# A long-convolution branch run between the matmuls of a gated MLP: its k·v transform shares a slot with an inverse transform, and its slots are dealt anew

## The chip, the core and the metric

The kernel runs on one core of a Trainium2 chip. The time is the device time of one execution in microseconds. Before the change it is 1860.31 us, the median of three runs (1859.35 to 1860.98).

## What is computed

Forward and backward pass of a layer with two branches over S = 2048 rows and D = 1024 channels, in bf16:

```python
xn = layernorm(x)
# A: a gated long convolution along the rows, one channel at a time
k_shift = sum(k_pad[:, t:t+S] * shift_k[:, 3-t] for t in range(4))      # four taps
kv = k_shift * v
y  = irfft(rfft(kv, 2S) * rfft(ssm_k, 2S))[:S] + kv * ssm_D
# B: a gated MLP, F = 3584
h  = relu(xn @ W_gate) * (xn @ W_up)
out = x + xn * y + h @ W_down
```

The outputs are `out` and its gradients for x, k, v, the four taps, ssm_k, ssm_D and the three weights.

## The kernel before

**Two branches on one TensorE.** Branch B (class `LnMlp`) is a sequence of matmuls of 128x128 weights by 512 columns, called large matmuls here: `hidden` (gate, up and the gradient of h: three GEMMs of 8 large matmuls for each tile of 128 rows, 14 blocks of eight row tiles), then `grad_down` and `grad_in` (weight gradients, GEMMs of 16), `out_phase` and `grad_x`. Twice, in the first block of `grad_down` and at the seam to `grad_in`, `four` runs four GEMMs of 16 interleaved, so four accumulators are open at once; PSUM has eight tiles in all (`ps_tile`, a pool of 8).

**Branch A as slots.** Branch A (class `ABranch`) does the convolution and its gradients for eight groups of 128 channels. `slots` is a generator, written out by hand, that yields pairs: a piece of matmul work (or None) and a piece of VectorE work (or None). The main loop hands out large matmuls, and when `SLOT` = 1900 ns of them have been handed out (`DENSE` = 1900 or 1250 ns in `grad_down` and `grad_in`, the shorter one after a slot without matmuls) it places the next slot. All of it is kept in program order on every engine, so what stands first in a queue runs first.

**What a group does.** Transforms are done as two matrix steps with a 32x32 block transpose on VectorE between them (`flip`, two instructions of 128x1024). First steps are `fwd1` and `fwd1_filter` (eight matmuls for half of the row tiles' columns, 512 columns each, on 32-row tiles of the array, written into PSUM tiles `ps_c`); second steps are `f2`, `f2_pair`; inverses are `inv_a`, `inv_a_pair` (four quarters for a pair of spectra) and then `inv_b`. Every PSUM tile is cast by ScalarE (`act`, L87) into the arena. `cmul` is a complex product of two spectra, ten VectorE instructions. `taps` computes the four taps in seven VectorE steps. `inv_b` needs the flip of what the inverse wrote; `f2_pair` of the next group needs the flips of both its inputs (`flip_B`).

**Crossed blocks.** `joint` issues jobs of different row tiles in turn, so that they run side by side in the array. `crossed` puts two row tiles of an inverse and the two others of a forward first step into one such block, and the reverse into a second one. Before the change it is used for the filter's first step (with `inv_a`) and for the gated gradient's, `Bg` (with quarters 0 and 1 of `inv_a_pair`). The k·v first step, `f1k`, stands alone as two blocks at the end of a group.

**Loads.** `fetch` queues a load, one queued load is issued on SP's queue after each slot (`steps`), none while `hold` is set in the last rows of a block, and `need` issues at once. The stores of B's results (`ru`, `ht`) are deferred by two GEMMs (`defer`, `tick`) and issued on the same queue. The pools `e2` (tiles `ru`) and `e1` (`ht`, `gh`) have six buffers each.

Of the kernel before, what the change touches and what calls it, by code (L numbers as in the profile page):

```python
# [48 lines left out]
class ABranch:  # L49
# [59 lines left out]
    def open(self):  # L109
        R = "right"  # L110
        self.con = self.pool("a_con", 1, side=R)
        self.lng = self.pool("a_lng", 1, side=R)
        self.ld = self.pool("a_ld", 1, side=R)
        self.ts = self.pool("a_ts", 3, side=R)
        self.tmp = self.pool("a_tmp", 2, side=R)
        self.xp = self.pool("a_xt", 1, side=R)
        self.sm = self.pool("a_sm", 2, side=R)
        self.big = self.pool("a_big", 3, side=R)
        self.lnx = self.pool("a_lnx", 5, side=R)

    def open_arena(self):
        for _ in range(2):
            self.pools.pop().release()
        arena = self.pool("a_are", 1, side="right").tile([P, 8, NB1 * P], BF16, name="arena")
        self.flp = arena[:, 0:2, :].rearrange("p e (k c) -> p e k c", c=P)
# [6 lines left out]
        self.Bh = arena[:, 6, :].rearrange("p (b x cp n i) -> p b x cp n i", x=2, cp=16, n=NB1, i=2)  # L132
        self.Bg, self.Bk, self.H, self.GKV = rows(7), rows(6), spectrum(4), spectrum(7)
        self.Cg, self.Ch, self.Cy = half(5), half(5), half(6)
# [6 lines left out]
    def tables(self):  # L141
# [28 lines left out]

        it = self.ts.tile([P, 2, NB1], I32, name="itR", tag="ts")
        tr = self.ts.tile([P, 2, NB1], F32, name="trR", tag="ts")
        hold(nc.gpsimd.iota(it[:], pattern=[[0, 2], [4, NB1]], base=1, channel_multiplier=0))
# [24 lines left out]
        V.tensor_scalar(out=wI[:], in0=itW[:], scalar1=q32[:], scalar2=None, op0=ALU.add)  # L198
        itN = self.ts.tile([P, 1, NB1], F32, name="itN", tag="ts")
        itNi = self.ts.tile([P, 1, NB1], I32, name="itNi", tag="ts")  # L200
        hold(nc.gpsimd.iota(itNi[:], pattern=[[0, 1], [1, NB1]], base=0, channel_multiplier=0))
# [49 lines left out]
    def store_time(self, ap2d, cg, t):  # L251
        for u in range(2):
            self.store(self.tview(ap2d, cg)[u], t[64 * u:64 * u + 64, 0:16, :])

    def ttile(self, name):
        return self.ts.tile([P, 19, P], BF16, name=name, tag="ts")

# [12 lines left out]
    def load_filter(self, st):  # L270
        st["hn"] = self.ld.tile([P, 2, 32, NB1], BF16, name="hn")
        self.load_rows(st, 0)
        self.later(self.load_rest, st)
# [15 lines left out]
    def load_xn(self, st):  # L289
        xt = st["xt"] = self.xp.tile([P, 16, P], BF16, name="xt")  # L290
        self.load_time(xt, self.xn_d, st["cg"])
# [4 lines left out]
    def load_k(self, st):  # L296
        nc = self.nc
        kp = st["kp"] = self.lng.tile([P, 19, P], BF16, name="kp")
        self.pri.now()
        self.tc.keep_in_program_order(nc.gpsimd.memset(kp[0:1, 0:3, :], 0.0))  # L300
        kv = self.tview(self.k, st["cg"])
        self.load_time(kp[:, 3:19, :], self.k, st["cg"])
        self.load(kp[64:P, 0:3, :], kv[0, :, 13:16, :])
        self.load(kp[1:64, 0:3, :], kv[1, 0:63, 13:16, :])
# [189 lines left out]

    def crossed(self, inv, fwd):

        I, F = inv[0], fwd[0]
        return [self.joint(I[0][0:1], I[1][0:1], F[2], F[3]), self.joint(F[0], F[1], I[2][0:1], I[3][0:1])] + inv[1][1:]

# [75 lines left out]
    def steps(self):  # L575
# [12 lines left out]
        yield 3400  # L588
        self.load_k(st)
        self.load_taps(st)  # L590
        yield 3400
        self.load_g(st)
        yield 3400
        self.load_v(st)
        yield 6800
        self.load_xn(st)
        self.pin = False
        self.pri.strict = True
        self.open_arena()
        self.begin(st)  # L600
        for st in self.sts:
# [15 lines left out]
    def start_kvt(self, st):  # L617
        kvt = st["kvt"] = self.ttile("kvt")
        self.tt(kvt[:, 0:16, :], st["ksh"][:], st["vt"][:], ALU.mult)

# [18 lines left out]
    def first(self, st):  # L639
        tk, f1h, nx = st["tk"], self.fwd1_filter(st)[1], self.ahead(st, 1)  # L640
        yield f1h[0], None
        yield None, tk
        yield f1h[1], tk
        self.fetch(nx, self.load_filter)
        yield None, self.both(lambda: self.add_D(st), tk)
        yield None, tk
        flH = self.flip_H()
        yield None, flH
        yield None, flH
        yield None, tk  # L650
        yield None, tk
        f2H = [(1, self.f2(self.H, 1, j)) for j in range(4)]
        yield f2H[0:2], lambda: self.gate_grad(st)
        self.fetch(nx, self.load_xn)
        yield None, tk
        yield f2H[2:4], lambda: self.start_kvt(st)
        yield None, None
        f1g, f1k = self.fwd1(self.Bg, st["gt"])[1], self.fwd1(self.Bk, st["kvt"])[1]
        yield f1g[0], None
        yield None, None  # L660
        yield f1g[1], None
        self.fetch(nx, self.load_g)
        yield None, None
        yield f1k[0], None
        flG = self.flip_B(self.Bg, 0)
        yield None, flG
        yield f1k[1], flG
        yield None, None
        flK = self.flip_B(self.Bk, 1)
        yield None, flK  # L670
        yield None, flK
        yield None, None

    def slots(self, st, gi):
# [28 lines left out]
        if last:  # L703
            iaG = [iaG[1][0], None, iaG[1][1]]
        else:
            self.need(self.load_filter, nx)
            self.need(self.load_rest, nx)
            iaG = self.crossed(iaG, self.fwd1_filter(nx))
        yield iaG[0], q
# [3 lines left out]
        yield None, lambda: self.turn(H, 1, 1)  # L713
        self.fetch(n2, self.load_filter)
        q = self.cmul(K, G, True, G, 0)
# [27 lines left out]
        yield [], lambda: self.halo(st)  # L743
        self.fetch(nx, self.load_k, self.load_taps)
        ia = self.inv_a_pair()
        if last:
            ia = [ia[1][0], None] + ia[1][1:]
        else:
            self.need(self.load_xn, nx)
            yield None, lambda: self.gate_grad(nx)  # L750
            self.fetch(n2, self.load_xn)
            ia = self.crossed(ia, self.fwd1(self.Bg, nx["gt"]))
        yield None, None
        q = self.cmul(K, G, True, G, 1)
        yield ia[0], q
        yield None, q
        yield None, q
        yield ia[1], q
        yield None, q
        q = self.cmul(H, K, False, K, 1)  # L760
        self.fetch(n2, self.load_g)
        yield None, q
        yield ia[2], q
        yield None, q
        yield None, q
        yield None, q
        gk = self.ttile("gk")
        tg = self.taps(st, gk, gks, [(0, 0), (1, 1), (2, 2), (3, 3)])
        yield None, tg
        yield None, tg  # L770
        yield ia[3], tg
        yield None, tg
        yield ia[4], tg
        yield None, tg
        f2H = [] if last else [(1, self.f2(H, 1, j)) for j in range(4)]
        yield f2H[0:2], tg
        self.store_time(self.out_gk, st["cg"], gk)
        fly = self.flip_C(self.Cy, 0)
        yield None, fly
        yield None, fly  # L780
        tk = None
        if not last:
            self.need(self.load_k, nx)
            self.need(self.load_taps, nx)
            self.begin(nx)
            tk = nx["tk"]
        yield None, tk
        yield None, tk
        yield f2H[2:3] + self.inv_b(st, "yt", 0), tk
        self.store_time(self.y_d, st["cg"], st["yt"])  # L790
        flh = self.flip_C(self.Ch, 0)
        yield None, flh
        yield None, flh
        yield None, tk
        yield None, tk
        yield f2H[3:4] + self.inv_b(st, "gh", 0), tk
        yield None, tk
        yield None, None
        if last:
            yield None, lambda: self.store_gh(st)  # L800
            return
        self.need(self.load_v, nx)
        yield None, lambda: self.start_kvt(nx)
        f1k = self.fwd1(self.Bk, nx["kvt"])[1]
        yield None, lambda: self.store_gh(st)
        flG = self.flip_B(self.Bg, 0)
        yield f1k[0], None
        yield None, flG
        yield f1k[1], flG
        yield None, None  # L810
        flK = self.flip_B(self.Bk, 1)
        yield None, flK
        yield None, flK
        yield None, None
        yield None, None
# [4 lines left out]
class LnMlp:  # L820
# [7 lines left out]
    def open_left(self):  # L828
# [3 lines left out]
        self.w2 = tc.alloc_tile_pool(name="b_w2", bufs=1, side="left")  # L832
        self.e2 = tc.alloc_tile_pool(name="b_e2", bufs=6, side="left")
        self.e1 = tc.alloc_tile_pool(name="b_e1", bufs=6, side="left")
        self.ps = tc.alloc_tile_pool(name="b_ps", bufs=8, space=bass.MemoryType.PSUM)
# [978 lines left out]
```

## Time and profile before

| | |
|---|---|
| median of three runs | 1860.31 us |
| the profiled execution | 1859.57 us, its span 1857.8 us |
| TensorE busy | 1836.3 us (99%), granted clock 1.00 |
| VectorE busy | 1114.7 us (60%) |
| VectorE busy in 475 to 635 us (`hidden` with A) | 130.43 of 160 us |
| VectorE busy in 880 to 1000 us (`grad_in` with A) | 82.88 of 120 us |
| ScalarE busy | 646.0 us (35%) |
| flip, 128x1024 f32 | 1934 ns each, 96 of them |
| product of 128x2048 bf16 on VectorE | 1219 ns |
| cast of a `ps_c` tile | 609 ns, 576 of them |
| a large matmul | 379 ns shown |

The span is of one execution. The duration of a matmul is modelled and overlaps the next one: large matmuls of one GEMM start 0.216 us apart (eight of them take 1.89 us in the timeline, which is seven spacings and one duration). A few matmul records are missing from the trace, so a run of 16 may be shown as 15.

### The profile page before, as it was taken

What the parts mean: (1) busy time and instruction counts of PE and PEld (TensorE: products, weight loads), DVE (VectorE), ACT (ScalarE), POOL (GpSimd) and SP (SyncE); (2) the same over time, 40 slices, a digit from 0 to 9 for tenths busy, and PEclk for the clock granted to TensorE, in tenths of its full rate; (3) what the DMA queues carried; (4) which work ended last, traced back from release to release, by engine and by line L of the source; (5) the groups of instructions that cost most, each with busy time, mean ns of one, the idle gap of its engine ahead of it and who ended that gap; (6) DMA issues with size and microseconds to landing.
All of it is one profiled execution on the core that took longest, in us unless ns stands there. A gap on an engine that the chain in (4) does not pass through costs nothing.

```text
span 1857.8 us, 31871 instructions
## 1 busy us (share of the span) xinstructions
PE 1836.3 (99%) x12840; PEld 844.2 (45%) x13061; DVE 1114.7 (60%) x1635; ACT 646.0 (35%) x1215; POOL 19.2 (1%) x51
## 2 busy tenths in 40 slices
PE   9999999999999999999999999999999999999999
PEld 4444444444444444444444444444444544444444
DVE  6656888798698777685585874801222222466652
ACT  5645444444545445544545454320000000111100
POOL 1000000000000000000000000000000000000000
PEclk9999999999999999999999999999999999999999
DMA  9898499779559838368474363488999857799973
GB/s 266 246 238 184 130 226 226 191 172 208 151 145 242 251 91 213 118 159 259 120 184 132 110 183 110 136 222 235 252 243 254 184 141 166 177 210 213 206 151 74
DMA packets 748132, 344.65 MB, mean 186 GB/s; under 512 B 576088, under 2 KB 715344, under 8 KB 747984
## 3 DMA queue, kind: packets, MB, share of 16 engines
q1 hardware_dynamic: 736848, 320.31, 71.2%
q10 hardware_dynamic: 9504, 17.04, 2.9%
q0 software_dynamic: 1632, 5.24, 0.8%
q8 instruction: 102, 1.67, 0.4%
q14 instruction: 46, 0.38, 0.1%
HBM read 143.79 MB, written 103.83 MB: 133 GB/s over the span
## 4 chain that ended last, share of the span: by engine, by line
PE 97%; issue 1%; DVE 1%; DMA 1%; ACT 0%; SPq 0%; DVEq 0%; ACTq 0%
PE ps_x L1666 21%; PE ps_w L1370 20%; PE ps_h L1035 10%; PE ps_g L1035 10%; PE ps_u L1035 10%; PE ps_o L1534 10%; PE ps_d L1370 9%; PE ps_c L83 4%; PE ps_d L1386 1%; PE ps_w L1386 1%; PE ps_r L1568 0%; DMA wu<-in_B_W_up_dram 0%; PE pst_x L1074 0%; DMA ugs<-ug_d 0%; DMA ln_x<-in_A_q_dram 0%
## 5 line engine op out<-in xcount | busy, mean ns | idle before, releaser
L1370 PE MATMUL ps_w<-ugs,xn_nat 128*128 128x512 bf16 x1673 | 376.0, 379 | 4.4 <-issue 2.4
L87 ACT CAST arena<-ps_c 128x512 bf16<-128x512 f32 x576 | 294.7, 609 | 76.5 <-PE ps_c L83 76.2
L1035 PEld LDWEIGHTS <-xnT 128*128 128x128 bf16 x1792 | 171.6, 98 | 210.7 <-issue 8.2
L332 DVE STREAM_TRANSPOSE arena<-arena 128x1024 f32<-128x1024 f32 x96 | 179.9, 1934 | 128.1 <-ACT arena L87 109.8
L1370 PEld LDWEIGHTS <-xn_nat 128*128 128x128 bf16 x1728 | 165.0, 98 | 201.8 <-issue 8.1
L1035 PE MATMUL ps_u<-wu,xnT 128*128 128x512 bf16 x873 | 205.0, 379 | 1.7 <-DMA wu<-in_B_W_up_dram 0.2
L1035 PE MATMUL ps_g<-wg,xnT 128*128 128x512 bf16 x871 | 204.4, 379 | 2.0 <-DVE xnT L1079 0.3
L1035 PE MATMUL ps_h<-wdT,goT 128*128 128x512 bf16 x867 | 203.0, 379 | 2.3 <-DVE ru L1150 0.7
L1666 PE MATMUL ps_x<-wgT,ggT 128*128 128x512 bf16 x879 | 197.5, 379 | 0.9
L1666 PE MATMUL ps_x<-wuT,guT 128*128 128x512 bf16 x877 | 197.4, 379 | 1.0
L1684 ACT ACTIVATE w<-xn,m 128x512 f32<-128x512 bf16 x32 | 24.3, 806 | 479.9 <-DVE m L1677 366.6
L1534 PE MATMUL ps_o<-wd,hT 128*128 128x512 bf16 (+1 forms) x878 | 186.6, 372 | 0.9
L1370 PE MATMUL ps_d<-g_nat,hs 128*128 128x512 bf16 x740 | 167.9, 379 | 1.9 <-issue 0.8
L1666 PEld LDWEIGHTS <-guT 128*128 128x128 bf16 x896 | 87.7, 98 | 105.7
L1666 PEld LDWEIGHTS <-ggT 128*128 128x128 bf16 x896 | 87.7, 98 | 105.5
L1278 ACT CAST gh<-ps_h 128x512 bf16<-128x512 f32 x112 | 66.4, 593 | 195.1 <-PE ps_h L1035 188.4
L1035 PEld LDWEIGHTS <-goT 128*128 128x128 bf16 x896 | 86.2, 98 | 104.3 <-issue 2.5
L1534 PEld LDWEIGHTS <-hT 128*128 128x128 bf16 x896 | 87.7, 98 | 99.9
L1373 ACT CAST wi<-ps_w 128x512 bf16<-128x512 f32 x108 | 64.4, 596 | 190.0 <-PE ps_w L1370 158.9
L1526 DVE TENSOR_TENSOR ya<-ya,xe 128x1024 bf16<-128x1024 bf16 x16 | 11.1, 693 | 185.0 <-DMA xe<-xn_d 185.0
L1150 DVE SCALAR_TENSOR_TENSOR ru<-ru,ps_u 128x512 bf16<-128x512 bf16 x112 | 76.4, 682 | 66.0 <-PE ps_u L1035 41.7
L91 DVE TENSOR_TENSOR t<-arena 128x2048 bf16<-128x2048 bf16 x96 | 113.8, 1219 | 0.5
(145 smaller groups left out, 1378.8 us busy)
## 6 DMA issues: line engine op xcount, KB each, us to landing
ugs<-ug_d SPq DMA_DIRECT2D x112, 256.0 KB
ug_d<-ru SPq DMA_DIRECT2D x110, 256.0 KB
wg<-in_B_W_gate_dram SPq DMA_DIRECT2D x56, 256.0 KB
wu<-in_B_W_up_dram SPq DMA_DIRECT2D x56, 256.0 KB
hs<-h_d SPq DMA_DIRECT2D x56, 256.0 KB
out_dram<-wi SPq DMA_DIRECT2D x56, 256.0 KB
h_d<-ht SPq DMA_DIRECT2D x108, 128.0 KB
gt<-in_grad_out_dram SPq DMA_DIRECT2D x32, 256.0 KB
```

What stands on the lines that cost most here:

```text
L83: self.pri.pin(self.nc.tensor.matmul(out, lhsT=lhsT, rhs=rhs, start=start, stop=stop))
L87: self.pri.pin(self.nc.scalar.copy(out=out, in_=in_))
L91: self.pri.pin(self.nc.vector.tensor_tensor(out=out, in0=in0, in1=in1, op=op))
L332: self.pri.pin(self.nc.vector.transpose(out=df[:, c0:c0 + 32, :], in_=sf[:, c0:c0 + 32, :]))
L1035: self.pri.pin(self.nc.tensor.matmul(ps[:], lhsT=xT[:, kt * P:(kt + 1) * P], rhs=w(kt), start=(kt == 0), stop=(kt == self.DT - 1)), always ...
L1150: return self.pri.pin(nc.vector.scalar_tensor_tensor(out=ru[s][:, 1, :], in0=ru[s][:, 0, :], scalar=0.0, in1=ps[:], op0=ALU.is_gt, op1=ALU ...
L1278: self.pri.pin(nc.scalar.copy(out=gh[:], in_=ps[:]))
L1370: self.pri.pin(self.nc.tensor.matmul(ps[:], lhsT=lhsT(st), rhs=rhs(st), start=(st == 0), stop=(st == self.ST - 1)))
L1373: self.pri.pin(self.nc.scalar.copy(out=out, in_=ps[:]))
L1386: self.pri.pin(self.nc.tensor.matmul(ps[i][:], lhsT=lhsT(i, st), rhs=rhs(i, st), start=(st == 0), stop=(st == self.ST - 1)))
L1534: nc.tensor.matmul(ps, lhsT=hT[:, kt, :], rhs=self.wd[:, kt, oc], start=(kt == 0), stop=(kt == self.FT - 1))
L1666: nc.tensor.matmul(ps, lhsT=T[:, kt, :], rhs=W[:, kt, oc], start=(i == 0), stop=(i == n - 1))
```

## The change

- `crossed` now takes one quarter, so any quarter can be crossed. The k·v first step of the next group is crossed with quarter 3 of the inverse pair, in the group before, and its two blocks at the end of a group go. Quarter 0 is still crossed with `Bg`; quarters 1 and 2 stand alone, quarter 1 now ahead of the crossed block.
- To make that possible the taps of the next group's k (`begin`, `tk`) and the product k·v (`start_kvt`) come earlier, ahead of this group's own gradient taps (`tg`), which move behind them to the places between the last flips.
- `Bk` gets a ninth plane of the arena of its own; the filter tile `hn`, the tile `kp` of k and the product k·v share one buffer (tag `hk`), which is loaded with the filter, then with k, then overwritten by the product.
- `load_k` and `load_taps` are queued after the filter's first step, and `load_filter` of the group after next only after the second crossed block of k·v.
- The tiles of `ttile` have fixed buffers (`HOME`) instead of rotating through three; `e1` and `e2` have five buffers each.
- The first group's opening (`first`) is in a new order: the gradient's first step before the taps of k, and k is loaded there.

Over the program the blocks of small matmuls on TensorE go from 141 to 133, with the same number of matmuls.

```diff
-        arena = self.pool("a_are", 1, side="right").tile([P, 8, NB1 * P], BF16, name="arena")
+        arena = self.pool("a_are", 1, side="right").tile([P, 9, NB1 * P], BF16, name="arena")
...
-        self.Bg, self.Bk, self.H, self.GKV = rows(7), rows(6), spectrum(4), spectrum(7)
+        self.Bg, self.Bk, self.H, self.GKV = rows(7), rows(8), spectrum(4), spectrum(7)
...
+    HOME = dict(gkv=0, gks=1, gv=2, gk=0, yt=2, gh=1)
+
     def ttile(self, name):
-        return self.ts.tile([P, 19, P], BF16, name=name, tag="ts")
+        return self.ts.tile([P, 19, P], BF16, name=name, tag="ts%d" % self.HOME[name])
...
     def load_filter(self, st):
-        st["hn"] = self.ld.tile([P, 2, 32, NB1], BF16, name="hn")
+        hn = self.lng.tile([P, 19, P], BF16, name="hn", tag="hk")[:, 0:16, :].rearrange("p r c -> p (r c)")
+        st["hn"] = hn.rearrange("p (h c n) -> p h c n", h=2, n=NB1)
...
-    def crossed(self, inv, fwd):
+    def crossed(self, I, F, k):
 
-        I, F = inv[0], fwd[0]
-        return [self.joint(I[0][0:1], I[1][0:1], F[2], F[3]), self.joint(F[0], F[1], I[2][0:1], I[3][0:1])] + inv[1][1:]
+        I = [g[k:k + 1] for g in I]
+        return [self.joint(I[0], I[1], F[2], F[3]), self.joint(F[0], F[1], I[2], I[3])]
...
     def start_kvt(self, st):
-        kvt = st["kvt"] = self.ttile("kvt")
-        self.tt(kvt[:, 0:16, :], st["ksh"][:], st["vt"][:], ALU.mult)
+        st["kvt"] = st["kp"][:, 0:16, :]
+        self.tt(st["kvt"], st["ksh"][:], st["vt"][:], ALU.mult)
...
         yield iaG[1], q
         yield None, lambda: self.turn(H, 1, 1)
-        self.fetch(n2, self.load_filter)
+        self.fetch(nx, self.load_k, self.load_taps)
...
         yield [], lambda: self.halo(st)
-        self.fetch(nx, self.load_k, self.load_taps)
-        ia = self.inv_a_pair()
-        if last:
-            ia = [ia[1][0], None] + ia[1][1:]
-        else:
+        ia, inv = self.inv_a_pair()
+        q = self.cmul(K, G, True, G, 1)
+        yield inv[1], q
+        for _ in range(4):
+            yield None, q
+        q = self.cmul(H, K, False, K, 1)
+        cross, gk = [inv[0], None], None
+        if not last:
             self.need(self.load_xn, nx)
             yield None, lambda: self.gate_grad(nx)
             self.fetch(n2, self.load_xn)
-            ia = self.crossed(ia, self.fwd1(self.Bg, nx["gt"]))
+            cross = self.crossed(ia, self.fwd1(self.Bg, nx["gt"])[0], 0)
+        yield None, q
         yield None, None
...
+            self.begin(nx)
             tk = nx["tk"]
-        yield None, tk
-        yield None, tk
-        yield f2H[2:3] + self.inv_b(st, "yt", 0), tk
+            yield None, tk
+            yield inv[2], tk
+            yield None, tk
+            yield None, tk
+            yield f2H[0:2], tk
+            yield None, tk
+            yield None, tk
+            self.need(self.load_v, nx)
+            yield None, lambda: self.start_kvt(nx)
+            cross = self.crossed(ia, self.fwd1(self.Bk, nx["kvt"])[0], 3)
+            yield None, None
+        gk = self.ttile("gk")
+        tg = self.taps(st, gk, gks, [(0, 0), (1, 1), (2, 2), (3, 3)])
+        yield cross[0], tg
+        yield None, tg
+        yield None, None
+        yield cross[1], tg
+        self.fetch(n2, self.load_filter)
+        yield None, tg
+        yield None, tg
+        fly = self.flip_C(self.Cy, 0)
+        yield None, fly
+        yield None, fly
+        yield None, tg
+        yield f2H[2:3] + self.inv_b(st, "yt", 0), None
         self.store_time(self.y_d, st["cg"], st["yt"])
         flh = self.flip_C(self.Ch, 0)
         yield None, flh
         yield None, flh
-        yield None, tk
-        yield None, tk
-        yield f2H[3:4] + self.inv_b(st, "gh", 0), tk
-        yield None, tk
-        yield None, None
+        yield None, tg
+        self.store_time(self.out_gk, st["cg"], gk)
+        yield f2H[3:4] + self.inv_b(st, "gh", 0), None
...
-        self.need(self.load_v, nx)
-        yield None, lambda: self.start_kvt(nx)
-        f1k = self.fwd1(self.Bk, nx["kvt"])[1]
-        yield None, lambda: self.store_gh(st)
         flG = self.flip_B(self.Bg, 0)
-        yield f1k[0], None
         yield None, flG
-        yield f1k[1], flG
-        yield None, None
+        yield None, self.both(lambda: self.store_gh(st), flG)
         flK = self.flip_B(self.Bk, 1)
         yield None, flK
         yield None, flK
-        yield None, None
         yield None, None
...
-        self.e2 = tc.alloc_tile_pool(name="b_e2", bufs=6, side="left")
-        self.e1 = tc.alloc_tile_pool(name="b_e1", bufs=6, side="left")
+        self.e2 = tc.alloc_tile_pool(name="b_e2", bufs=5, side="left")
+        self.e1 = tc.alloc_tile_pool(name="b_e1", bufs=5, side="left")
```

## The prediction

> **What bounds the kernel now.** I read the busy shares and the chain on the page first.
>
> ```profile
> PE 1836.3 (99%) x12840; PEld 844.2 (45%) x13061; DVE 1114.7 (60%) x1635; ACT 646.0 (35%) x1215; POOL 19.2 (1%) x51
> PE 97%; issue 1%; DVE 1%; DMA 1%; ACT 0%; SPq 0%; DVEq 0%; ACTq 0%
> ```
>
> TensorE (PE) is the bound, with almost no gap. A time saved must therefore be a time of small blocks on PE or one of its few waits, and any slot whose VectorE (DVE) work isn't done when PE comes to it costs at once. Then the waits on PE, where two belong to branch A's overload of DVE:
>
> ```profile
> PE ps_h L1035 <- DVE ru L1150: 0.7, 1, 0.7
> PE ps_g L1035 <- DVE ru L1150: 0.2, 1, 0.2
> ```
>
> Then the timeline around the crossed block of before and around a first step that stands alone, for the price of a block:
>
> ```profile
> 709.17 0.30 PE L83 MATMUL ps_c<-arena,IA 32*64 32x256 bf16 x4
> 709.18 0.41 PE L83 MATMUL ps_c<-gt,R 32*64 32x512 bf16 x4
> ...
> 709.74 5.35 PE L1370 MATMUL ps_d<-g_nat,hs 128*128 128x512 bf16 x23
> 715.02 0.64 PE L83 MATMUL ps_c<-arena,IA 32*64 32x256 bf16 x32
> 715.60 7.08 PE L1370 MATMUL ps_d<-g_nat,hs 128*128 128x512 bf16 x31
> ...
> 996.64 0.42 PE L83 MATMUL ps_c<-kvt,R 32*64 32x512 bf16 x8
> 996.99 3.63 PE L1370 MATMUL ps_w<-ugs,xn_nat 128*128 128x512 bf16 x15
> ```
>
> The reader is to see the time from a block's start to the next large matmul, 0.57 crossed, 0.58 for a quarter alone, 0.35 for a first step alone. A block's price is this plus 0.309 (last large matmul's start to the block's) less 0.216 (the spacing it replaces): 0.663, 0.668 and 0.448.
>
> Last, the second steps of group 1, with what DVE must do between them:
>
> ```profile
> 453.06 1.07 ACT L87 CAST arena<-ps_c 128x512 bf16<-128x512 f32 x2 [0.26 <-PE ps_c L83]
> 454.02 2.07 ACT L87 CAST yt<-ps_c 128x512 bf16<-128x512 f32 x4
> ...
> 455.93 0.65 ACT L1278 CAST gh<-ps_h 128x512 bf16<-128x512 f32 x1
> ...
> 456.62 0.69 DVE L1279 TENSOR_TENSOR ru<-ru,gh 128x1024 bf16<-128x1024 bf16 x1 [1.02 <-ACT gh L1278]
> 457.22 3.71 DVE L332 STREAM_TRANSPOSE arena<-arena 128x1024 f32<-128x1024 f32 x2
> ...
> 463.31 0.25 PE L83 MATMUL ps_c<-arena,FW 64*32 64x128 bf16 x8
> 463.38 0.61 PE L83 MATMUL ps_c<-arena,RB 64*32 64x512 bf16 x16
> ...
> 464.82 1.45 PE L1035 MATMUL ps_h<-wdT,goT 128*128 128x512 bf16 x5 [0.66 <-DVE ru L1150]
> ```
>
> The casts, one product that stands ahead in DVE's queue, and two flips (0.65 to 0.69 and 3.71) end at 460.93; the RB part that reads them starts at 463.38. That margin of 2.45 us is what the new order spends.
>
> **The crossing.** For a middle group before: two crossed blocks, three quarters alone, two first steps alone, 2x0.663 + 3x0.668 + 2x0.448 = 4.226. After: four crossed, two alone, 3.988. 0.238 x 7 groups = 1.67. One group's spectrum step was cut into four blocks of 32 small matmuls (0.656 each, 2.624); it is now three (48, 48, 32: 0.874 + 0.874 + 0.656). 0.22. Together −1.89. Bounds: 0 and twice that.
>
> **Waits that go.** The blocks at 463.3 and 619.6 cost 1.605 and 1.142 where one of their kind without a wait costs 0.874: 0.73 and 0.27. The slots before them hold other DVE work in the new order: −1.00 (bounds 0 and −1.0).
>
> **Waits that come.** I walk the changed order of each queue with the rows of before. On DVE an instruction that needs nothing from the one ahead starts 0.08 before its end, a dependent one 0.03 after; casts of `ps_c` start 0.48 apart on ScalarE (ACT); PE's last matmul to the reader's start is 0.416; engine to engine some 0.06. Large matmuls are counted at 0.216 from a common point.
>
> *After the gh block's flips, group 0 (in `hidden`).* Between the yt block and the gh block 32 large matmuls stand in the new order instead of 48, since the taps' slots leave. By the row above, 16x0.216 = 3.46 less than a margin of 2.45: −1.0, a wait of 1.0. Queued behind the waiting RB matmuls is all of PE. Group 1 has one more product (0.61) ahead of the flips: 1.6.
>
> *Quarter 1 now ahead of the crossed block, group 0.* The block reads the product K·G right after it is made. Before, the last K part was written by 245.71 (244.42 + 1.29) and the block started at 249.83, a margin of 4.1 us. Now the taps' slots that stood ahead are gone and the GEMM's end starts a row of DVE work without a pause: 6 masks 0.682, 6 `ht` 0.425, 5 products with gh 0.687, 4 flips 1.934, 2 adds 0.199, 4 products 0.685, 4 sums 0.692, 1.219 for t, 2 tap products 1.218, 3 arena writes 0.684; overlaps (26x0.082 off, 11x0.034 on) leave 28.9 us. PE comes there after 128 large matmuls and one block, 28.2 us. A wait of 0.8, and 0.5 more for the other half of K: 1.3.
>
> *First spectrum step of group 1.* Forty large matmuls after the row's GEMM of the gradient of h PE is there; counted from DVE's first instruction behind that point, 40x0.216 + 0.309 − 0.416 = 8.5 us. DVE has a mask, an `ht`, 2 products and the four flips of G and K: 0.682 + 0.425 + 1.374 + 7.736, less 0.46 of overlaps, 9.8 us. Wait 1.3. Group 2 comes out even.
>
> *Group 4, the gh block's four flips* (3x1.85 + 1.934) against 32 large matmuls: 0.5.
>
> *In `four`, first time.* Eight of a block's RB matmuls are cut off behind two large ones, as PSUM tiles must come back from ACT's casts: 0.27 + 0.46 = 0.7.
>
> *In `four`, at the seam.* Three of the crossed blocks now fall where four accumulators are open. Four of eight PSUM tiles are left and a crossed block writes six (two inverse, four first step). A tile comes back 0.416 + 0.61 after its last matmul, the next 0.48 later, while PE needs the fifth after some 0.4. The worst comes to 0.93 + 0.45, the other two, which find a cast already under way, to 0.23 and 0.46: 2.1. Before, no crossed block stood inside `four`, so nothing bounds this directly; the ends are 0 and three full waits, 4.1.
>
> Sum 1.0 + 1.6 + 1.3 + 1.3 + 0.5 + 0.7 + 2.1 = 8.5. The same walk on the two waits of before gives 0.82 and 0.34 where the trace has 0.73 and 0.27, so it overstates by some 0.08 each; a dozen waits, 1.0 off: +7.5. Bounds: each DVE walk may be 0.25 us late or early, and an ACT cast may slip; 3.5 to 11.
>
> **What the skill says of it.** The Trainium skill, "TensorEngine Tiling (Array Packing)", section "PSUM Bottleneck", says that packing speeds up the array and not the reading of PSUM, so copies out may become the limit; this speaks against packing first steps together. The row: crossed blocks of before show no wait at 709.17, though six casts at 0.48 last 2.9 us against 0.57 of the block. An estimate by the rule alone would let each of the 14 added crossed blocks wait up to 2.3 us, 32 in all; by the row only those in `four` wait, as summed above. I go by the row.
>
> **First group, loads and buffers.** The load of k (four issues, 3.85 us of SP's queue in before) now stands ahead of the first up-weights there, which were issued at 132.86 to 135.3 and first used at 140.69. Issued some 2 us later, they keep 6.1 us. Landing times of other loads and stores in the trace are 4.0 to 6.1 us. Cost 0 to 1.2, taken 0.3. The clearing of the tile's pad on POOL moves with it; POOL is busy 1% and holds nothing up. The filter's load is queued later, behind the second crossed block of k·v; to its use are 184 large matmuls, 40 us: nothing, and without that cover its one landing of some 6 us. Five buffers: a product with gh waits for the store of the tile five back instead of six; the margin is a microsecond or more, the stores on SP take 0.55 to 1.35 each. Once in before ACT waits 2.8 us for such a store, hidden beside PE. At 0, up to 3 if SP's queue is held by loads. The adds of fixed buffers (`HOME`) move no instruction.
>
> **The sum.** −1.89 − 1.00 + 7.5 + 0.3 = +4.9 on the profiled execution of 1859.57, 1864.5. The median of three is 0.74 above that execution: 1865.2.
>
> **Rivals.** *The waits are covered* (the other side). If DVE arrives earlier than walked, by 0.25 us or more at each place, waits of 1.3 turn into 1.0, and those in `four` may vanish because ACT is only 35% busy. With all gone, 1860.31 − 1.89 − 1.00 = 1857.4. It decides for not slower where the waits sum to less than 6.3 (4.9 − 7.5 + 6.3 = 3.7, the bound of what a measurement tells, 0.2%). For: DVE is at 60%; against: 130 of 160 us busy in `hidden`, where four of these places lie. *Loads and stores are late too.* Weights late in the first group and stores held by five buffers add 2 to 7: 1867 to 1872. For: SP's queue is one queue for all; against: no wait of PE on a store in before. *The crossing saves nothing* because four row tiles of mixed shapes run as long as two blocks: +1.9, 1867; against it, the 0.57 above, the same mix measured.
>
> **The numbers.** Waits as walked 0.60, covered 0.20, loads too 0.17, no saving 0.03. Slower by over 0.2% (3.7 us, about what a measurement of this kernel can tell from no change) means above 1864.0: two thirds of the main case, 0.40, and all of the two slow rivals, 0.20, give 0.60. Covered in full, with a block's saving at the upper bound, ends below 1856.6: a quarter of that rival, faster 0.05. The rest, same, 0.35. The main case alone is 1861 to 1868.5; with the upper part of the covered case and the lower part of late loads the range is 1859.5 to 1869.5, which leaves a tenth out on each side.
>
> **What would show it.** Right: in the timeline of after a crossed k·v block of about 0.57 us to the next large matmul; PE waits on `ps_c` from DVE flips near the gh blocks of groups 0 and 1, on the K write before quarter 1, and on ACT casts within `four`. Wrong: fewer than four such waits, or waits of PE on weights' loads, or on stores of `ru`. The sum of PE's idle before DVE and ACT, now about 1, should be near 7.5.

## The result, and the profile after

The changed kernel takes 1865.27 us (median of 12 runs, 1863.99 to 1866.90) against 1860.24 us for the kernel before (12 runs). The ratio is 1.0026, with a 95% interval from 1.0017 to 1.0035. The forecast was 1865.2 us, slower by 0.26%. The profiled execution has a span of 1863.7 us, 5.9 more than before.

The busy shares and the chain of the changed kernel:

```profile
PE 1836.8 (99%) x12842; PEld 846.2 (45%) x13061; DVE 1112.2 (60%) x1635; ACT 646.7 (35%) x1215; POOL 19.3 (1%) x51
PE 72%; issue 1%; DVE 0%; DMA 0%; ACT 0%
```

The busy time of PE and of DVE is that of before within 2.5 us. Nothing was added to the work, so 5.9 us more can only be idle time of PE. The chain is followed back from the end only to the flip at 481.63 us that PE waits for in group 1's gh block and the product ahead of it (481.11), where the view finds nothing that released it; so its shares sum to 73%, and those of before to nearly the whole span. The waits on PE of the changed kernel (us in total, times, the longest):

```profile
PE ps_c L83 <- DVE arena L334: 3.1, 4, 1.2
PE ps_d L1389 <- DMA g_nat<-in_grad_out_dram: 1.0, 3, 0.4
PE ps_c L83 <- ACT arena L87: 0.8, 2, 0.6
PE ps_c L83 <- DVE arena L91: 0.7, 2, 0.5
```

The two waits on `ru` of before are gone, and PE's small blocks wait for the flips (L334), for the arena writes (L91) and for the casts (L87). The view counts only the time behind the modelled end of the last matmul. A block's price, from start to start as in the prediction, says what PE loses. The k·v block that is now crossed, in PE's timeline of the changed kernel:

```profile
297.88 0.30 PE L83 MATMUL ps_c<-arena,IA 32*64 32x256 bf16 x4
297.89 0.41 PE L83 MATMUL ps_c<-kp,R 32*64 32x512 bf16 x4
298.01 0.39 PE L83 MATMUL ps_c<-arena,IA 32*64 32x256 bf16 x8
298.13 0.38 PE L83 MATMUL ps_c<-kp,R 32*64 32x512 bf16 x4
298.23 0.28 PE L83 MATMUL ps_c<-arena,IA 32*64 32x256 bf16 x4
298.45 1.90 PE L1038 MATMUL ps_g<-wg,xnT 128*128 128x512 bf16 x7
```

From 297.88 to 298.45 it is 0.57 us, a price of 0.663, as the crossed gradient block had before. The reader sees quarters and first step side by side, with no gap. The gh block of group 0 and the spectrum block after it, in the same timeline:

```profile
324.28 0.25 PE L83 MATMUL ps_c<-arena,FW 64*32 64x128 bf16 x8
324.35 0.38 PE L83 MATMUL ps_c<-arena,RB 64*32 64x512 bf16 x2
325.39 0.62 PE L83 MATMUL ps_c<-arena,RB 64*32 64x512 bf16 x14 [0.66 <-DVE arena L334]
...
337.63 0.85 PE L83 MATMUL ps_c<-arena,FW 64*32 64x256 bf16 x48 [0.99 <-DVE arena L334]
```

ACT and DVE in that stretch:

```profile
318.44 2.07 ACT L87 CAST yt<-ps_c 128x512 bf16<-128x512 f32 x4
320.36 0.65 ACT L1281 CAST gh<-ps_h 128x512 bf16<-128x512 f32 x1
...
321.04 0.69 DVE L1282 TENSOR_TENSOR ru<-ru,gh 128x1024 bf16<-128x1024 bf16 x1 [1.98 <-ACT gh L1281]
321.65 3.68 DVE L334 STREAM_TRANSPOSE arena<-arena 128x1024 f32<-128x1024 f32 x2
```

DVE stands idle for 1.98 us at a product that waits for a cast on ACT (to 321.01), which is behind the four casts of `yt`. The two flips don't need that cast: the inverse that they turn was finished by the crossed block at 303.73. But they are queued behind the product. They end at 325.33, and the RB matmuls go on at 325.39. At the spectrum block of group 1 the price is 1.936 where 0.874 is without a wait.

The crossed blocks at the seam meet ACT's casts. At 846, in PE's timeline:

```profile
846.04 0.39 PE L83 MATMUL ps_c<-arena,IA 32*64 32x256 bf16 x8
847.00 0.89 PE L83 MATMUL ps_c<-gt,R 32*64 32x512 bf16 x4 [0.57 <-ACT arena L87]
```

Price by price, the waits against the walk of the prediction:

| place (us in the changed kernel) | walked | measured |
|---|---|---|
| quarter 1 of group 0 (250) | 1.3 | 1.680 − 0.668 = 1.01 |
| gh block, group 0 (324) | 1.0 | 1.919 − 0.874 = 1.05 |
| first spectrum step, group 1 (337) | 1.3 | 1.936 − 0.874 = 1.06 |
| gh block, group 1 (482) | 1.6 | 2.501 − 0.874 = 1.63 |
| cut block in `four`, first time (645) | 0.7 | 0.75 |
| crossed blocks in `four`, seam (838 to 867) | 2.1 | 0.21 + 1.35 + 0.51 = 2.07 |
| first spectrum step, group 5 (after the gh block of group 4; 897) | 0.5 | 0.27 |
| loads of `g_nat` (647 to 649) | – | 1.0 |
| sum | 8.5, taken as 7.5 | 7.8 and 1.0 |

In the cut block and the two crossed blocks at 846 and 867 a record of a large matmul is missing behind the block, which shows as 0.226 more; it is taken off (at 645: 0.885 + 1.185 − 0.226, against 1.095 for the block that was cut in the same way in before; at 846: 2.236 − 0.226 − 0.663 = 1.35; at 867: 1.398 − 0.226 − 0.663 = 0.51). The 0.21 is the step in the starts of the weight loads of the two traces behind the block at 838.

The first step of the filter also became dearer: most of its crossed blocks cost 0.777 instead of 0.752, ten more than before, 0.26 in all. The start of the program is 0.17 later. The sum, −1.89 − 1.00 + 7.8 + 1.0 + 0.26 + 0.17 = 6.3, compares with 5.98 us, by which the last weight load of a large matmul is later than in the trace of before. Most of the difference, 0.2, is a wait for up-weights in before that is gone as well.

### The profile page after: what moved, and what is told of

Read it like the earlier page. It is cut to its first block, busy times and chain, and to the rows that moved or that the text cites. A ratio compares the mean times of both kernels' runs of the same rounds, so it can differ in the third digit from the quotient of the medians.

```text
span 1863.7 us, 31858 instructions
## 1 busy us (share of the span) xinstructions
PE 1836.8 (99%) x12842; PEld 846.2 (45%) x13061; DVE 1112.2 (60%) x1635; ACT 646.7 (35%) x1215; POOL 19.3 (1%) x51
## 3 DMA queue, kind: packets, MB, share of 16 engines
q8 instruction: 102, 1.67, 0.4%
## 4 chain that ended last, share of the span: by engine, by line
PE 72%; issue 1%; DVE 0%; DMA 0%; ACT 0%
PE ps_x L1669 21%; PE ps_w L1373 20%; PE ps_o L1537 10%; PE ps_d L1373 9%; PE ps_c L83 3%; PE ps_u L1038 3%; PE ps_h L1038 3%; PE ps_g L1038 2%; PE ps_d L1389 1%; PE ps_w L1389 1%; DVE arena L334 0%; PE ps_r L1571 0%; DMA g_nat<-in_grad_out_dram 0%; ACT arena L87 0%; ACT wi L1413 0%
## 5 line engine op out<-in xcount | busy, mean ns | idle before, releaser
L87 ACT CAST arena<-ps_c 128x512 bf16<-128x512 f32 x576 | 293.9, 610 | 103.5 <-PE ps_c L83 103.3
L334 DVE STREAM_TRANSPOSE arena<-arena 128x1024 f32<-128x1024 f32 x96 | 179.6, 1930 | 134.7 <-ACT arena L87 114.2
L91 DVE TENSOR_TENSOR t<-arena 128x2048 bf16<-128x2048 bf16 x96 | 113.9, 1218 | 0.4
```

Of the source, the lines that this page charges most:

```text
L87: self.pri.pin(self.nc.scalar.copy(out=out, in_=in_))
L91: self.pri.pin(self.nc.vector.tensor_tensor(out=out, in0=in0, in1=in1, op=op))
L334: self.pri.pin(self.nc.vector.transpose(out=df[:, c0:c0 + 32, :], in_=sf[:, c0:c0 + 32, :]))
```

## Experiments

**The crossing alone.** The k·v first step uncrossed, in the same slots:

```diff
-            cross = self.crossed(ia, self.fwd1(self.Bk, nx["kvt"])[0], 3)
+            f1k = self.fwd1(self.Bk, nx["kvt"])[1]
...
-        yield cross[0], tg
-        yield None, tg
+        yield (cross[0] if last else inv[3]), tg
+        yield (None if last else f1k[0]), tg
         yield None, None
-        yield cross[1], tg
+        yield (cross[1] if last else f1k[1]), tg
```

> The changed kernel with only the k·v first step uncrossed again: in the same slots quarter 3 stands alone and the first step's two halves follow as blocks of their own. Theory (a crossed block saves what the blocks' prices say): per group 2 blocks of 0.663 become 0.668 + 2 x 0.448, +0.238, in 7 groups +1.67; the wait of about 0.5 us of the crossed k·v block inside the four open accumulators (at 866.9 us) goes, so +1.2 in all, a span of about 1864.9 against 1863.7. Rival (crossing saves nothing): no change from the blocks, and 0.5 less from the wait, about 1863.2.

Measured: 1867.32 us, 1.0043 of before (1.0026 to 1.0060), a span of 1865.0, 1.3 more than the changed kernel. The blocks cost what their prices said: in PE's timeline

```profile
303.73 0.42 PE L83 MATMUL ps_c<-kp,R 32*64 32x512 bf16 x8
304.08 1.90 PE L1038 MATMUL ps_g<-wg,xnT 128*128 128x512 bf16 x8
```

a first step alone takes 0.35 to the next large matmul; the fourteen of them have a mean price of 0.447, and quarter 3 costs 0.668. That gives the 1.67. The wait of 0.51 at the crossed k·v block of the seam went, but a second gradient block in `four` now waits 1.35, the same as the first, and the loads of `g_nat` 0.6 less. So by the blocks' prices the crossing saves what was forecast, and the change was slower in spite of it. The time alone doesn't tell that: the interval overlaps that of the changed kernel (1.0017 to 1.0035), and waits moved as well.

**The waits for DVE.** One of the two flips ahead of the gh blocks of groups 0 and 1 left out (so gh of these two groups is not the reference's), and in group 0 the product for the gradient of v, with its store, moved behind quarter 1:

```diff
-        yield None, lambda: self.tt(gv[:, 0:16, :], gkv[:, 0:16, :], st["ksh"][:], ALU.mult)
+        mk_gv = lambda: self.tt(gv[:, 0:16, :], gkv[:, 0:16, :], st["ksh"][:], ALU.mult)
+        yield None, (None if gi == 0 else mk_gv)
...
-        yield None, None
+        yield None, (None if gi else mk_gv)
...
-        yield None, flh
+        yield None, (None if gi < 2 else flh)
         yield None, flh
```

> The changed kernel without the second of the two flip instructions ahead of the gh block in groups 0 and 1 (left out: half of that block transpose, so gh of two groups is not the reference's), and with the product for the gradient of v of group 0 moved from before quarter 1 to behind it. Theory (the RB matmuls of the gh block wait for VectorE's flips, and quarter 1 for VectorE's chain): the waits of 1.05 and 1.63 us at 324 and 482 go, that of 1.01 us at 250 falls by 1.2 less overlap to nothing or 0.2; the wait of 1.06 at 337.6 stays since PE and VectorE come earlier there by the same amount; -3.5 in all. Rival (PE waits there for the casts of the yt block and PSUM tiles, and the profile only names the last semaphore): -1.0 or less.

Measured: 1862.01 us, 1.0011 of before (1.0002 to 1.0021), a span of 1859.9, 3.8 less than the changed kernel. The same two blocks in its timeline:

```profile
323.83 0.25 PE L83 MATMUL ps_c<-arena,FW 64*32 64x128 bf16 x8
323.89 0.61 PE L83 MATMUL ps_c<-arena,RB 64*32 64x512 bf16 x16
324.32 0.35 PE L83 MATMUL ps_c<-arena,FW 64*32 64x128 bf16 x24
...
336.12 0.85 PE L83 MATMUL ps_c<-arena,FW 64*32 64x256 bf16 x48 [0.98 <-DVE arena L334]
```

The gap between the second and the third RB matmul is gone, and so are the waits at 482 and 250; the one at 336 stays at 1.05, as foretold. So at these three places, 3.7 us together, PE waits for DVE's work and not for the casts of the block ahead or for PSUM tiles.

**The waits inside `four`.** In group 4 alone, gradient and k·v blocks taken apart:

```diff
-            cross = self.crossed(ia, self.fwd1(self.Bg, nx["gt"])[0], 0)
+            fg = self.fwd1(self.Bg, nx["gt"])
+            cross = [inv[0], fg[1][0], fg[1][1]] if gi == 4 else self.crossed(ia, fg[0], 0)[0:1] + [None] + self.crossed(ia, fg[0], 0)[1:]
...
-            cross = self.crossed(ia, self.fwd1(self.Bk, nx["kvt"])[0], 3)
+            fk = self.fwd1(self.Bk, nx["kvt"])
+            cr = self.crossed(ia, fk[0], 3)
+            cross = [inv[3], fk[1][0], fk[1][1]] if gi == 4 else [cr[0], None, cr[1]]
```

> The changed kernel with the crossed gradient and k·v blocks of group 4 alone (those that lie in or by the four open accumulators of the seam) taken apart into a quarter and two halves of the first step, each four PSUM tiles. Theory (a crossed block wants six tiles where four are free, and waits for ACT's casts): the waits of 1.35, 0.51 and 0.21 us go, the blocks cost 2 x 0.238 = 0.48 more, -1.6. Rival (the casts are the limit whatever the blocks are, since the same twelve tiles of each pair are cast): waits of the same size at the plain blocks, about +0.5.

Measured: 1864.84 us, 1.0028 of before (1.0016 to 1.0040), a span of 1863.4, against 1863.7. The k·v pair lost its 0.51 and the wait of 0.21 went, but this says little of the theory, as the halves of the k·v first step now come at 871.02 and 873.21, at the end of `four`. The gradient pair waits as before:

```profile
844.93 0.42 PE L83 MATMUL ps_c<-gt,R 32*64 32x512 bf16 x8
845.29 0.60 PE L1394 MATMUL ps_d<-g_nat,hs 128*128 128x512 bf16 x2
846.01 1.87 PE L83 MATMUL ps_c<-gt,R 32*64 32x512 bf16 x8
847.82 2.55 PE L1394 MATMUL ps_d<-g_nat,hs 128*128 128x512 bf16 x11
```

The two halves come only two large matmuls apart here (1.1 us), and each writes four tiles. ACT gives a tile back each 0.48 us, so the second half is drawn out to 1.81 us, a wait of 1.64. This fits a limit on the number of tiles asked for within a microsecond or two while four accumulators are open; other distances between the halves weren't tried. The crossed block asks for six at once, but it isn't the only way to run into the casts.

**The late loads.** The stores of the last two gradients of `ru` moved to POOL's queue:

```diff
-                    queue = nc.gpsimd if n == 0 and s < 2 else nc.sync
+                    queue = nc.gpsimd if n == 0 and s < 2 or last and s >= HS - 2 else nc.sync
```

> The changed kernel with the stores of the last two row tiles' gradients of the last hidden block issued on POOL's queue instead of SP's. Theory (the last four loads of g_nat were issued at 642.1 instead of at about 637.5 because SP stood at the store of ru, whose product on VectorE came behind a flip): the three waits on g_nat, 1.0 us in all, go: -1.0. Rival (the tiles that g_nat is loaded into come free late, or the landing is what is slow): the three waits stay, 0.

Measured: 1865.60 us, 1.0031 of before (1.0019 to 1.0042), a span of 1862.7. Two waits of 0.6 us together are left. The last four `g_nat` loads on SP's queue, in the changed kernel and in this one:

```profile
642.10 2.05 SPq L1068 DMA_DIRECT2D g_nat<-in_grad_out_dram  x4
```

```profile
639.32 4.63 SPq L1068 DMA_DIRECT2D g_nat<-in_grad_out_dram  x4
```

The first of them was issued 2.8 us earlier, but the four took 4.63 us instead of 2.05, and the fourth came at 643.53 instead of 643.76. So the edit hardly brought the loads forward, and it doesn't settle whether the stores are what makes PE wait. In the three kernels above, without this edit, the wait was 0.4, 0.6 and 0.3, so it also varies from one profile to the next by as much as the edit could bring. In before, where these loads were issued at 635.6, there was none. Why they come late stays open.

**Five buffers, by themselves.** The kernel before with `bufs=5` in both pools:

> The kernel before with five buffers instead of six in both pools, as in the changed kernel. Theory (the sixth buffer covers nothing): the same time as before within 0.7 us, no wait of PE that was not there. Rival (products and masks wait for stores of the tile five back): 1 to 3 us more.

Measured: 1859.51 us, ratio 0.9998 (0.9989 to 1.0007). In the order of before the sixth buffer covers nothing that PE waits for, though ACT's waits for stores of `ru` and `ht` rise from 2.8 to 11.7 us.

**Are the waits local?** One idle slot ahead of the gh block in groups 0 and 1:

```diff
+        if gi < 2:
+            yield None, None
         yield f2H[3:4] + self.inv_b(st, "gh", 0), None
```

> The changed kernel with one idle slot ahead of the gh block in groups 0 and 1 alone. If each wait is local: those of 1.05 and 1.63 us there go, -2.7. If the slots are phased to the rows of the gated MLP (every later slot of these and the following groups comes eight large matmuls later against the GEMMs that give VectorE its masks and products): the two waits fall, but new ones come at other blocks, and the time is not less than that of the changed kernel.

Measured: 1873.68 us, 1.0071 of before (1.0052 to 1.0089), 8.4 above the changed kernel. The two waits fell from 1.05 and 1.63 to 0.27 and 0.87, and these came in their place:

```profile
PE ps_g L1040 <- ACT ru L1148: 4.6, 1, 4.6
PE ps_c L83 <- DVE arena L334: 2.9, 4, 2.0
PE ps_c L83 <- DVE arena L91: 1.2, 4, 0.4
```

All later slots come eight large matmuls later against the rows of the gated MLP, and other blocks meet DVE's work: at 507 a spectrum block costs 2.99 where 0.874 is without a wait. The wait of 4.6 us for ACT is of a kind that the changed kernel doesn't have at all. Giving one wait room thus cost more than the wait. A part of the 8.4 is clock: behind the wait of 4.6 us, at 353.6, the granted clock is 0.5 for 3.4 us (more of this in the next run).

**Room for all of them.** Eleven idle slots, at places chosen with the walk of the prediction carried on through all groups (the pair is group and number of the slot that the idle one precedes; slots of group 0 start behind 26 of its opening):

```diff
+    IDLE = {(0, 60): 1, (0, 95): 1, (0, 96): 1, (1, 0): 1, (1, 30): 1, (1, 75): 1, (2, 56): 1, (2, 61): 1, (4, 26): 1, (4, 44): 1, (4, 47): 1}
...
-            for p, d in self.slots(st, st["gi"]):
+            for k, (p, d) in enumerate(self.slots(st, st["gi"])):
+                for _ in range(self.IDLE.get((st["gi"], k), 0)):
+                    if self.queue and not self.hold():
+                        self.issue()
+                    yield self.DENSE[1] if self.dense else self.SLOT
```

> The changed kernel with eleven more idle slots and nothing else: in group 0 one ahead of quarter 1 and two ahead of the gh block, three in group 1, two in group 2, three in group 4 by the seam. Theory (the new time is waits of PE for VectorE and for casts, 7.6 us, and the crossing saves what the blocks' prices say): the waits at 250 (1.01), 324 (1.05), 337 (1.06), 482 (1.63), 645 (0.74) and 897 (0.27) go, those by the four open accumulators of the seam fall from 2.1 to about 1.2; -6.6, a span of about 1857.1 and a time just below that of the kernel before. Rival (VectorE's work is only put off, and PE waits for it at the next place): a gain of 2 or less, a span above 1861.

Measured: 1864.25 us, 1.0022 of before (1.0013 to 1.0031), a span of 1863.0. The gain of 6.6 that was forecast didn't come. All the waits named went, those at the seam fell to 1.05 at one crossed block (1.713 − 0.663 at 862), but 4.1 us came in a new place:

```profile
PE ps_g L1043 <- ACT ru L1151: 2.8, 1, 2.8
PE ps_c L83 <- ACT gh L1286: 1.3, 1, 1.3
```

ACT's own waits in the same kernel, and SP's queue ahead of the place:

```profile
ACT ru L1151 <- DMA ug_d<-ru: 13.7, 4, 6.0
ACT gh L1286 <- DMA h_d<-ht: 5.8, 1, 5.8
```

```profile
334.02 3.74 SPq L99 DMA_DIRECT2D hn<-in_A_ssm_k_dram  x2
337.85 1.19 SPq L1292 DMA_DIRECT2D ug_d<-ru  x1
339.10 2.04 SPq L99 DMA_DIRECT2D hn<-in_A_ssm_k_dram  x2
341.24 1.10 SPq L1169 DMA_DIRECT2D h_d<-ht  x1
```

The cast of gh waits 5.8 us for a store of `ht` that still reads the tile, issued at 341.24. Ahead of that store the loads of the filter hold SP's queue for 5.8 us. Whether six buffers would take the wait away was not tried. With the two stores of the last rows on POOL too:

> The kernel with the eleven idle slots, and the stores of the last two row tiles of the last hidden block on POOL's queue. Theory (the g_nat loads wait behind those stores on SP): the waits on g_nat, 0.3 to 1.0 in the runs so far, go, 0.5 less than with the idle slots alone. Rival (they are late for another reason): the same as with the idle slots alone.

Measured: 1862.92 us, 1.0019 of before (1.0010 to 1.0028), a span of 1860.4, with the same 4.2 us at 343 to 350. The kernel without this edit had no wait on `g_nat` either, so the run doesn't speak for the theory. Of the 2.6 us between the two spans 1.5 are in the sixteen matmuls behind the wait for ACT, here without the edit and then with it:

```profile
350.21 5.07 PE L1043 MATMUL ps_g<-wg,xnT 128*128 128x512 bf16 x16 [2.77 <-ACT ru L1151]
```

```profile
349.95 3.61 PE L1043 MATMUL ps_g<-wg,xnT 128*128 128x512 bf16 x16 [2.91 <-ACT ru L1151]
```

In a window from 349.8 to 353.2 the granted clock is 0.50 in the first and 1.00 in the second (behind the window and its length stand the busy times of PE, PEld, DVE, ACT and POOL, then the granted clock, the DMA share and GB/s):

```profile
349.80:353.20 3.40, 2.99 (x8) 1.03 (x8) 0.00 (x0) 3.29 (x7) 0.00 (x0) 0.50 1.00 353
```

```profile
349.80:353.20 3.40, 3.25 (x16) 1.45 (x15) 0.00 (x0) 3.40 (x8) 0.00 (x0) 1.00 0.99 348
```

In the slowed stretch large matmuls start 0.427 apart instead of 0.216. So a long wait of PE can be followed by a further loss of some 1.5 us; the other differences between the two kernels are in waits for loads.

**What holds ACT there.** On top of that kernel, in group 0 the stores of branch A on POOL's queue, and the filter of group 2 loaded behind the gh block:

```diff
-            self.store(self.tview(ap2d, cg)[u], t[64 * u:64 * u + 64, 0:16, :])
+            self.pri.late()
+            queue = self.nc.gpsimd if cg.start == 0 else self.nc.sync
+            self.pri.pin(queue.dma_start(out=self.tview(ap2d, cg)[u], in_=t[64 * u:64 * u + 64, 0:16, :]))
...
-        self.fetch(n2, self.load_filter)
+        if gi:
+            self.fetch(n2, self.load_filter)
...
+        if gi == 0:
+            self.fetch(n2, self.load_filter)
```

> The kernel with the eleven idle slots and the two stores on POOL, and for group 0 also its y, gk, gh and gradient-of-v stores on POOL's queue and the load of the filter of the group after next queued behind the gh block. Theory (the new wait of 4.1 us at 343 to 350 us comes from SP's queue: loads of hn and the store of gk stand ahead of the stores of ht and ru, and with five buffers ScalarE's casts wait for those): the wait goes, -4.1 against the kernel with idle slots and stores on POOL, a span of 1856.3 and a time of about 1858.5, below the kernel before. Rival (the products on VectorE are late there, and a store that is issued earlier would wait for them): the wait stays or falls by 1 at most.

Measured: 1864.14 us, 1.0020 of before (1.0011 to 1.0029), a span of 1860.8. The wait went from its place and came back 24 large matmuls later, 2.9 us before 354.67, behind the filter's loads, of which the last two now stood on SP from 345.35 to 349.31. (The clock was 0.5 for 3.4 us behind this wait too.) This points to the filter's load and not the stores of A as what the stores of `ht` and `ru` wait for. It was tried without the other edits of this run, on the kernel with the two stores on POOL:

```diff
-            self.load(st["hn"][64 * x:64 * x + 64, h], hv[x, h])
+            if st["gi"] == 2:
+                self.pri.now()
+                self.pri.pin(self.nc.gpsimd.dma_start(out=st["hn"][64 * x:64 * x + 64, h], in_=hv[x, h]))
+            else:
+                self.load(st["hn"][64 * x:64 * x + 64, h], hv[x, h])
```

> The kernel with the eleven idle slots and the two stores on POOL, with one more edit: the four DMAs that load the filter of group 2 go on POOL's queue instead of SP's (the other edits of the last run are not in it). Theory (with five buffers ScalarE waits for a store of ht or ru wherever about 4 us of filter loads stand ahead of it on SP; in the last run that was at 345 to 349, in the one before at 335 to 341): the wait of 4.1 us at 343 to 350 goes or falls below 1, a span of about 1856.5. Rival (VectorE is late there, and the loads only look like the cause): the wait stays at 3 or more, a span of 1859.5 or above.

Measured: 1859.00 us, 0.9994 of before (0.9985 to 1.0003), a span of 1857.7. The longest waits on PE that are left:

```profile
PE ps_w L1382 <- issue: 2.7, 17, 0.2
PE ps_u L1047 <- DMA wu<-in_B_W_up_dram: 1.9, 1, 1.9
PE ps_d L1382 <- issue: 1.7, 11, 0.2
PE pst_x L1086 <- DVE ln_x L946: 1.5, 1, 1.5
```

No flip, arena write or store stands in this list any more; by the prices one crossed block at 857 still waits 1.05 for tiles. The kernel is 6.3 us below the changed one by the medians, with the same crossed blocks; against the kernel before the interval takes in no change. The "issue" rows stand for missing matmul records, 0.2 each, and the wait of the first matmuls (1.5 here, 0.3 in the profile of before) varies between the profiles of these kernels from nothing to 1.5. One more try went for the 1.9:

```diff
-                    queue = nc.gpsimd if n == 0 and s < 2 or last and s >= HS - 2 else nc.sync
+                    queue = nc.gpsimd if n == 0 and s < 2 or s >= HS - 2 else nc.sync
```

> The last kernel (eleven idle slots, group 2's filter loads on POOL), with the stores of the gradients of the last two row tiles on POOL's queue in every hidden block and not only in the last. Theory (a store of ru on SP stood from 492.0 to 495.9 us for a product that VectorE has behind a flip, and the up-weights queued behind it came 1.9 us late): the wait of 1.9 us at 500 us goes, nothing else comes, span 1855.8 against 1857.7, and the time 0.1 to 0.2% below the kernel before. Rival (the longer landing of POOL's stores holds the five buffers): new waits of ScalarE for ru that reach PE, no gain.

Measured: 1865.68 us, 1.0030 of before (1.0020 to 1.0040). The wait for weights fell to 0.6, but the waits for ACT at 343 to 356 are back (2.3 and 1.5 us):

```profile
324.64 12.61 SPq L1071 DMA_TRANSPOSE goT<-in_grad_out_dram  x4
...
339.05 1.35 SPq L107 DMA_DIRECT2D y_d<-yt  x2
340.50 1.49 SPq L1173 DMA_DIRECT2D h_d<-ht  x1
```

The four transposing loads ahead of the stores held SP's queue for 12.61 us in this execution. In the kernel just before it they took 5.45:

```profile
324.35 5.45 SPq L1071 DMA_TRANSPOSE goT<-in_grad_out_dram  x4
```

The first store of `ht` behind them is issued at 340.50 instead of 335.03, and with five buffers that reaches PE. Behind these waits, from 351.8 on, the clock was again 0.5 for 3.4 us.

## Why the prediction was right

- *TensorE is the bound, and the time is its waits.* Right: PE's busy time didn't move, and taking away what it waits for takes the time away (1859.00 us with the crossing kept).
- *The crossing, −1.89.* Its 1.67 is shown by uncrossing the k·v first step: the blocks cost that much more, as priced. The one spectrum step in three blocks instead of four (0.22) also has the prices forecast.
- *Waits that go, −1.00.* Right: neither is in the list of after.
- *Waits that come, +7.5.* 7.8 by the blocks' prices, at the seven places that were named. That it came so near is in part luck. The walk gave 8.5; at quarter 1 of group 0 and at the first spectrum steps it overstated by 0.2 to 0.3 each, but at the gh blocks and in `four` it was right to 0.05, so the calibration from the two waits of before, which took off 0.08 for each, has about the right sum and the wrong spread. At quarter 1 the list of DVE's work as it is printed sums to 27.7 us, which is less than PE's 28.2; the 28.9 comes out with a second product for t, and the trace of the changed kernel has two there (238.34 and 241.14).
- *The sign that PE's idle before DVE and ACT would be near 7.5.* The view of waits shows only 4.6 (3.1 + 0.8 + 0.7). The 7.5 was reckoned in prices from start to start, and it is by prices that it came true.
- *In `four`, 2.1.* Size and places right; the reason given, that a crossed block writes six tiles, was too narrow, since two plain blocks of four tiles, close together, wait as long. Eleven of the fourteen crossed k·v blocks cost 0.663, two 0.889, which is 0.663 and a missing record, and only the one in `four` waits. The rule from the Trainium skill, "TensorEngine Tiling (Array Packing)", section "PSUM Bottleneck", says that copies out of PSUM may become the limit when the array is packed; applied to every added crossed block it would have let each of them pay. In this kernel the copies are the limit only where four of the eight tiles are held by other accumulators.
- *First group's loads, 0.3.* PE doesn't wait for the up-weights there, 0; issued from 136.78 on and first used at 142.69, they had a lead of 5.9 us.
- *Five buffers at 0.* Right for PE in the changed kernel and in the kernel before. The margin is used up on ACT, though: it waits 20.1 us for stores of `ru` and `ht` in the changed kernel, and 2.8 before, hidden beside PE. And it holds for these orders alone: in all kernels with idle slots but one, 2.9 to 4.6 us of such waits reached PE.
- *Left out of the sum:* the loads of `g_nat`, 1.0 in the profiled execution (a part of the rival of late loads), and 0.26 of dearer filter blocks. The sum was made for the profiled execution, and there it was 1.0 low (1864.5 against 1865.49). The median was met because 0.74 had been added for the distance of before's profiled execution from its median, while that of the changed kernel lies 0.22 above its own: luck.
- *The rival that the waits are covered* was refuted by the blocks' prices; that it would give 1857.4 is not far from the 1859.00 of the kernel with idle slots, where most of them are covered and 1.9 and 1.05 us of waits are left.

## To carry to other kernels

When one engine is 99% busy, price a block from start to start and look for what it will have to wait for, since 2 us saved on the engine are soon lost where a reader comes 16 matmuls sooner (1.05 us at the first such place here). Walk each queue in program order from the last common point: the item that holds it is often an unrelated one (a product behind a cast, a store behind a load). A gap opened at one place moves every later slot against the other branch, so after such a change the whole order has to be walked again.

## What the runs showed of the hardware that was not expected

- In four profiled executions (one idle slot ahead of the gh blocks of groups 0 and 1; the eleven idle slots alone; branch A's stores of group 0 on POOL; the last run) PE waited 2.3 to 4.6 us for ACT at some 347 to 355 us, and then the granted clock was 0.5 for 3.4 us, which costs 1.4 to 1.7 us more. In a fifth (1862.34 us) a wait of 2.9 us was followed by no such stretch. The changed kernel, whose longest wait on PE was 1.5 us at the start and 1.2 us behind it, had none. What decides wasn't tried.
- Four DMA_TRANSPOSE issues of the same kind held SP's queue for 5.45 us in one kernel and 12.61 us in another that differs in which queue some stores of `ru` use. In the one with 12.61, POOL issued four filter loads and two such stores at 318.7 to 324.5, just ahead of the transposing loads; in the other it issued the four filter loads at 305.6 to 310.0.
- A crossed block of an inverse and the filter's first step costs 0.752 or 0.777 us in one and the same program; before, one in fourteen cost the higher, after, eleven. Why wasn't tried.
- The wait for the loads of `g_nat` was 0.3 to 1.0 us in five kernels with the same matmul order at that place, one of them with two stores on another queue.
